# Gated products written in place in PSUM, and matrix comparisons moved to GpSimd, in an FNet plus PEER mixture-of-experts kernel

## The chip, the cores and the metric

The kernel runs on one core of a Trainium2 chip. A core has five engines that run their own instruction streams and meet at semaphores: TensorE (PE, with its weight loads shown as PEld), VectorE (DVE), ScalarE (ACT), GpSimd (POOL) and SyncE (SP, which here only issues DMAs). The measure is the device time of one execution in microseconds, lower being better.

## The reference

The kernel adds three things for 2048 tokens of width 512: the input, the real part of a two-dimensional Fourier transform of the layernormed input, and a mixture of 4096 one-row experts, of which every one of 32 heads picks two.

```python
def _A_ref(x, re_s, im_s, re_d, im_d):                 # FNet
    a = einsum("bsd,ed->bse", x, re_d); b = einsum("bsd,ed->bse", x, im_d)
    return einsum("ts,bse->bte", re_s, a) - einsum("ts,bse->bte", im_s, b)

def _B_ref(x, w_q, k1, k2, u, v):                      # PEER, K = 2, E = 64
    q = einsum("nd,dhc->nhc", xf, w_q)                 # 32 heads
    s1, s2 = q1 @ k1.T, q2 @ k2.T                      # 64 scores each
    # the two best of each half give four candidates, of which the two best are kept
    top_s, top_e = ...                                 # top_e = i1 * 64 + i2
    g = softmax(top_s)
    act = gelu(einsum("nd,nhkd->nhk", xf, u[top_e]))
    return einsum("nhk,nhk,nhkd->nd", g, act, v[top_e])

xn = layernorm(x)
return x + _A_ref(xn, ...) + _B_ref(xn, w_q, k1, k2, u, v)
```

The Fourier matrices are inputs. The kernel uses their symmetries to read only a part of them, so it also compares the parts it leaves out with the parts it uses, by subtracting mirrored pieces and summing absolute values; a flag at the end says whether the short way held. Another group of checks (`fit`) bounds the sizes of the expert tables, so that splitting them into two f16 halves is safe.

## The kernel before, in words

**First part (about 0 to 443 us).** Layernorm, the folded Fourier transform, the query product and the scores (line 796), and the top-two search on VectorE. Some of the matrix comparisons (numbers 8 to 23 and 40 to 51, the list `EARLY`) already lie here, on GpSimd. In this part the change only shifts line numbers.

**Expert part (about 443 to 1106 us).** The 2048 tokens are 16 tiles of 128. For 14 tiles, called blocks here, the kernel computes *all* 4096 experts densely and multiplies by a gate that is zero for experts that no head chose. The last two tiles are done by gathering only the chosen rows of the expert tables. One block b passes through these steps:

- `u_part` (line 956): z = u·x in eight groups (`cg` 0 to 7) of 48 matmuls into a PSUM tile. Groups 2 and 5 use the PSUM ring "pc", the others the ring "pb". ACT takes each group through gelu into the SBUF tile `act` (line 959).
- `g_mm` (lines 980 to 993): the gate of 32 tokens. VectorE builds two one-hot tiles `L` (line 980) and the weighted one-hot tile `R` (lines 988, 991), PE multiplies them (32 matmuls, line 993) into one PSUM gate tile `pg`. There are four such gates in a block (`tg` 0 to 3) and **two** `pg` buffers, so gate k+2 can be written only when gate k has been released.
- `w_part` (lines 1003 to 1016): VectorE multiplies `act`, a constant and the gate (line 1004) into the SBUF tile `w`. ACT rounds `w` to its f16 high half (line 1011), VectorE subtracts that from `w` for the low half (line 1014). High and low half replace `act` in place.
- `v_part` (line 1023): the eight groups of 12 matmuls that multiply the halves by the table v into one PSUM tile of the ring "pc"; `finish` (line 1038, VectorE) reads that tile into `y`, which frees it for group 2 or 5 of the next `u_part`.

A stage of PE is therefore: eight groups of z for block b with gates (b,0) and (b,1) among them, then eight groups of v for block b-1 with gates (b,2) and (b,3) among them. The small tables at the end of the program place the `w_part` steps: those of gates (b,0) and (b,1) go with groups 0 and 4 of v, those of (b,2) and (b,3) with groups 0 and 3 of the next z. The names z0 to z7 in this text are the groups of `u_part`; w0 to w3 the products of the four gates of a block, sub0 to sub3 the subtractions of line 1014, copy0 to copy3 the rounding of line 1011.

Three other chains are spread over these stages by counters (`pick` and `paced`), which issue a share of each list after each group of matmuls:

- the **row gathers** of the last two tiles: 128 steps, each an indirect DMA by POOL into a row buffer "ga" (line 1049, five buffers), a dot product on VectorE (line 1065), gelu and scaling on ACT (lines 1075, 1076, 1078), and an add on POOL (line 1083), after which POOL issues the next fetch into the freed buffer;
- the **late comparisons**: `compare` for the 36 numbers that are not in `EARLY`, and `compare_w` for four more. A comparison loads a 128x1024 tile "cx" by two SP DMAs, two steps later takes differences on VectorE (lines 739 to 773, by kind), and two steps after that ACT sums absolute values (lines 778, 780, called the judge below). Those with `g == 0` need a special treatment of row 0, hence extra small instructions on one partition;
- the `fit` checks on ACT (lines 1151, 1157).

The tiles "w", "cx" and "fit" of this part share one ring of four SBUF buffers (`WB`).

Every engine works strictly in the order of its own queue. That order is made by the scheduler of the framework out of the order in which the steps are written and their dependences.

Of the kernel before, what the change touches and what calls it, by code (L numbers as in the profile page):

```python
# [8 lines left out]
F32 = mybir.dt.float32  # L9
# [7 lines left out]
ALU = mybir.AluOpType  # L17
# [19 lines left out]
def tile_fnet_peer(ctx, tc, x, ca, cb, c5, wt, wf, wr, wq, kt, ut, vn, uv, out):  # L37
# [56 lines left out]
    early = cst.tile([P, len(EARLY)], F32, name="early")  # L94
    sums_sb = cst.tile([P, 138 + NF + 3], F32, name="sums")
    chk, asum = sums_sb[:, 0:70], sums_sb[:, 70:138]

# [3 lines left out]
    k16 = sums_sb[:, 0:128].bitcast(F16).rearrange("p (l w k) -> p l w k", l=2, w=2)  # L101
    fits = sums_sb[:, 138:]

# [452 lines left out]
    def part_b(safe, stS, stP, stE, xt, u_sb, cmp_p):  # L556
# [163 lines left out]
        def compare(n, at=None):  # L720
# [16 lines left out]
            def diff():  # L737
                if g == 0:
                    nc.vector.tensor_tensor(tv[:, 1], tv[:, 1], tv[:, 0], op=ops[0])
                    for i in (2, 3):  # L740
                        nc.vector.scalar_tensor_tensor(tv[:, i], tv[:, 0], not0, tv[:, i], op0=ALU.mult, op1=ops[i - 1])
                    f = (-1 if ri else 1) * sgn[1] * sgn[2]
                    nc.vector.tensor_tensor(tv[0:1, 3], tv[0:1, 3], tv[0:1, 2],
                                            op=ALU.subtract if f > 0 else ALU.add)
                else:
                    sets = {}
                    for i, o in enumerate(ops):
                        sets.setdefault(o, []).append(i + 1)
                    for o, ix in sets.items():
                        sl = slice(ix[0], ix[-1] + 1, ix[1] - ix[0] if len(ix) > 1 else 1)  # L750
                        v = tv[:, sl]
                        v_eng.tensor_tensor(v, v, tv[:, 0:1].to_broadcast([P, len(ix), 256]), op=o)
# [8 lines left out]

                if g == 0:
# [166 lines left out]
        TG = 32  # L929
        WB = 4  # L930
        BUFS = 5
        BT = [blk_tiles(b) for b in range(2)]
# [66 lines left out]
        def w_part(b, tg):  # L999
            act, _ = ACT[b]  # L1000
            ts = slice(tg * TG, (tg + 1) * TG)
            p = GP.pop((b, tg))
            w = bp.tile([P, NC, TG], F32, tag="w", name=f"w{b}_{tg}", bufs=WB)
            nc.vector.scalar_tensor_tensor(w, act[:, :, ts], fw,  # L1004
                                           p.rearrange("p h (n c) -> p c (h n)", c=NC),
                                           op0=ALU.mult, op1=ALU.mult)
            w16 = parts(b)[:, :, ts]
# [87 lines left out]
        def pick(after, k=1):  # L1095
            done[0] += k
            made = nc.cur_bb.bb.instructions
            for f in picks[done[1]:-(-len(picks) * done[0] // turns)]:
# [3 lines left out]
                for i in made[first:]:  # L1102
                    if i.engine in (mybir.EngineType.DVE, mybir.EngineType.Activation):
                        follow(i, after)
                    if i.engine == mybir.EngineType.Activation and after.ins.name in GL:
                        follow(i, GL[after.ins.name])

        def compare_w(n):

# [27 lines left out]
            if ri:  # L1137
                nc.scalar.activation(v[0][0:1, 0:P], v[0][0:1, 0:P], AF.Abs, accum_out=chk[0:1, 68 + half:69 + half])
            c = P - half
# [3 lines left out]
            f = t.rearrange("p k e -> p (k e)")[:, P - half * ri:]  # L1143
            after(2, lambda: nc.scalar.activation(f, f, AF.Abs, accum_out=chk[:, n:n + 1]))

# [16 lines left out]
        def verdict():  # L1162
# [3 lines left out]
            N = NF + 3  # L1166
            fm = sums_sb[:, 138 + NF:]
# [3 lines left out]
            cols = ((slice(0, 64), 50), (slice(64, 70), 47))  # L1171
            for i, (c, k) in enumerate(cols):
                nc.vector.tensor_reduce(fa[:, i:i + 1], asum[:, c.start:min(c.stop, 68)], axis=AX.X, op=ALU.add)
            nc.vector.tensor_scalar(bnd, bnd, -31.5, None, op0=ALU.add)
# [4 lines left out]
            follow(i.ins, T["a"])  # L1179
            k = nc.gpsimd.partition_all_reduce(fr[:, 2:], sums_sb[:, 138:], P, bass_isa.ReduceOp.absmax)  # L1180
            follow(k.ins, i)
# [39 lines left out]
        if not safe:  # L1221
            nc.vector.memset(chk[:, 68:70], 0.0)
            for k in range(0, len(EARLY), 16):
# [236 lines left out]
```

## Time and profile before

| what | us |
|---|---|
| median of three runs | 1119.79 (1116.18 to 1124.1) |
| profiled execution | 1113.87 |
| its span (first to last instruction) | 1112.1 |
| PE busy in the span | 1070.3 (96%) |
| VectorE busy | 996.7 (90%) |
| ACT busy | 717.7 (65%) |
| GpSimd busy | 640.3 (58%) |
| PE waiting for `y` (line 1038) | 15.5 |
| PE waiting for the gate product (line 1004) | 1.9 |

The profiled execution is 0.5% below the median. Busy times are sums over the whole span; the page of the profile also cuts the span into 40 slices, in which one reads that VectorE is at 0.9 or more of nearly every slice from 500 us on, and PE as well. A wait is put down to the instruction that ended it. Durations of matmuls are modelled, those of VectorE, ACT and POOL are records.

### The profile page before, as it was taken

To read this page: it belongs to the slowest core of one execution; us is meant where nothing else is said; L and a number is where in the kernel's file an instruction comes from. 1 tells how busy PE (TensorE), PEld (TensorE's weight loads), DVE (VectorE), ACT (ScalarE), POOL (GpSimd) and SP (SyncE) were. 2 spreads that over 40 slices of the span, in tenths; PEclk is the share of its full clock that TensorE was granted. 3 is DMA by queue.
4 is the path that set the end of the run, shared out by engine and by line. 5 is a ranking of instruction groups with operands and counts; after the bars stand their busy time and mean duration, and the time that the engine had idled before them with its cause. 6 is when DMAs were issued, how large, how long until landed. Compare 5 with 4: busy or idle time off the path is not lost. (4 is left out here: it accounts for less than half of the span.)

```text
span 1112.1 us, 28462 instructions
## 1 busy us (share of the span) xinstructions
PE 1070.3 (96%) x11070; PEld 700.6 (63%) x11070; DVE 996.7 (90%) x2786; ACT 717.7 (65%) x1324; POOL 640.3 (58%) x552
## 2 busy tenths in 40 slices
PE   5899999999999999999999999999998999999897
PEld 4355555454544544987695776968667686786853
DVE  6978897978999999987999999999999999998981
ACT  3576657778788767423766667767566666765660
POOL 0013537588797855211668677756666667667651
PEclk9899999999999999999999999999998999999899
DMA  8248153535446332553677577676767567776521
GB/s 326 83 172 284 49 198 113 173 125 198 153 153 206 106 114 65 186 158 109 186 213 238 193 212 231 225 232 201 215 199 209 182 214 237 230 222 189 158 67 51
DMA packets 84433, 196.72 MB, mean 177 GB/s; under 512 B 10294, under 2 KB 27069, under 8 KB 84288
## 3 DMA queue, kind: packets, MB, share of 16 engines
q1 hardware_dynamic: 63394, 123.49, 33.1%
q0 software_dynamic: 20736, 71.31, 21.8%
q8 instruction: 88, 1.44, 0.5%
q14 instruction: 57, 0.47, 0.1%
q10 hardware_dynamic: 158, 0.01, 0.0%
HBM read 177.68 MB, written 17.10 MB: 175 GB/s over the span
## 5 line engine op out<-in xcount | busy, mean ns | idle before, releaser
L796 PE MATMUL s<-m,xq 128*128 128x512 f16 x1536 | 338.9, 379 | 0.0
L956 PE MATMUL z<-xb,u 128*128 128x128 f16 x5376 | 313.9, 221 | 15.5 <-DVE y L1038 15.5
L956 PEld LDWEIGHTS <-u 128*128 128x128 f16 x5376 | 307.6, 99 | 19.2 <-issue 16.4
L1083 POOL TENSOR_TENSOR ov<-ov,ga 128x512 f32<-128x512 f32 x128 | 203.5, 1590 | 167.2 <-ACT ga L1078 145.7
L1023 PE MATMUL v<-v,act 128*128 128x512 f16 x1344 | 298.6, 379 | 0.0
L796 PEld LDWEIGHTS <-xq 128*128 128x128 f16 x1536 | 148.3, 98 | 171.4 <-issue 0.2
L1023 PEld LDWEIGHTS <-act 128*128 128x128 f16 x1344 | 128.3, 98 | 146.1
L1049 POOL DMA_INDIRECT ga<-in_uv_dram,eix x128 | 173.0, 1351 | 47.2 <-POOL ov L1083 34.2
L980 DVE TENSOR_TENSOR L<-io_lam,cmp 128x2048 f16<-128x2048 f16 x112 | 157.8, 1441 | 13.5 <-PE g L993 13.5
L804 DVE MAX8 vals<-ss 128x8 f32<-128x64 f32 x1024 | 152.4, 216 | 14.1 <-ACT ss L801 14.0
L959 ACT ACTIVATE act<-z,scl 128x512 f32<-128x512 f32 x112 | 75.8, 679 | 97.2 <-PE z L956 96.3
L808 DVE FIND_INDEX8 idx<-vals,ss 128x8 uint16<-128x256 f32 x256 | 107.1, 418 | 0.0
L801 ACT ACTIVATE ss<-s,wsc 128x512 f32<-128x512 f32 x112 | 75.5, 680 | 43.4 <-PE s L796 33.7
L1011 ACT ACTIVATE act<-w 128x1024 f16<-128x1024 f32 x56 | 75.5, 1348 | 43.3 <-DVE w L1004 39.8
L1078 ACT ACTIVATE ga<-ga,za 128x512 f32<-128x512 f32 x128 | 92.1, 721 | 9.8 <-ACT za L1076 0.4
L1014 DVE TENSOR_TENSOR act<-w,act 128x1024 f16<-128x1024 f32 x56 | 86.1, 1539 | 6.7 <-ACT act L1011 5.8
L778 ACT ACTIVATE cx<-cx 128x896 f32<-128x896 f32 x64 | 60.6, 946 | 40.3 <-DVE cx L758 12.9
L1065 DVE SCALAR_TENSOR_TENSOR ga<-ga,px 128x512 f32<-128x512 f32 x128 | 85.6, 676 | 0.1
L1004 DVE SCALAR_TENSOR_TENSOR w<-act,scl,g 128x1024 f32<-128x1024 f32 x56 | 70.9, 1271 | 0.4 <-ACT act L959 0.2
L169 POOL TENSOR_TENSOR wq<-wq,wh 128x1024 f16<-128x1024 f32 x26 | 55.4, 2134 | 24.4 <-ACT wq L166 23.7
L993 PEld LDWEIGHTS <-L 128*128 128x128 f16 x1792 | 52.2, 96 | 9.5 <-issue 2.7
L993 PE MATMUL g<-R,L 128*128 128x32 f16 x1792 | 54.0, 176 | 2.2 <-DVE w L1004 1.9
(274 smaller groups left out, 1312.4 us busy)
## 6 DMA issues: line engine op xcount, KB each, us to landing
cx<-in_cb_dram SPq DMA_DIRECT2D x64, 448.0 KB, 4.6
wq<-in_wq_dram SPq DMA_DIRECT2D x32, 512.0 KB, 5.8
fit<-in_wq_dram SPq DMA_DIRECT2D x28, 512.0 KB, 5.4
uv<-in_ut_dram SPq DMA_DIRECT2D x16, 512.0 KB, 4.1
uv<-in_vn_dram SPq DMA_DIRECT2D x16, 512.0 KB, 3.5
xq<-in_x_dram SPq DMA_DIRECT2D x8, 512.0 KB
xt_d<-xq SPq DMA_DIRECT2D x16, 256.0 KB, 3.0
cx<-in_ca_dram SPq DMA_DIRECT2D x64, 64.0 KB, 2.8
```

Source lines behind the costliest of these rows:

```text
L796: mm = nc.tensor.matmul(ps, xt[i][:, l, kd, :], m[:, r, kd, :], start=(n == 0), stop=(n == 3 * KD - 1))
L804: nc.vector.max(vals[:, i, w, :, h], s[:, g, :])
L808: nc.vector.max_index(idx[:, i, w].rearrange("p k h -> p (k h)"), vals[:, i, w, 0:2].rearrange("p k h -> p (k h)"), s[:, w * HC:g + 1, :]. ...
L956: mm = nc.tensor.matmul(p[:, cc * P:(cc + 1) * P], ug[:, l, c % 2, kd, :], xb[:, r, kd, :], start=(n == 0), stop=(n == 3 * KD - 1))
L980: nc.vector.tensor_tensor(L.rearrange("p t (l two) -> p t l two", two=2), io_lam.rearrange("p (l two) -> p l two", two=2).unsqueeze(1).to_ ...
L993: i = nc.tensor.matmul(p[:, hf, t * NC:(t + 1) * NC], L[:, t, :], R[:, hf * 16 + t, :], start=True, stop=True)
L1014: nc.vector.tensor_tensor(w16[..., 1], w, w16[..., 0], op=ALU.subtract)
L1023: mm = nc.tensor.matmul(pv, w16[:, c, :, l], vg[:, r, c % 2, :], start=(c == 0 and k == 0), stop=(c == NC - 1 and k == 2))
L1049: nc.gpsimd.indirect_dma_start(out=t, out_offset=None, in_=uv, in_offset=bass.IndirectOffsetOnAxis(ap=eix[:, n].rearrange("p k h -> p (k h ...
L1065: nc.vector.scalar_tensor_tensor(t, t, 1.0, T["x"], op0=ALU.mult, op1=ALU.mult, accum_out=T["z", n][:, s:s + 1])
L1078: nc.scalar.activation(t, t, AF.Copy, scale=z)
L1083: T["a"] = nc.gpsimd.tensor_tensor(o, o, t, op=ALU.add)
```

## The change

1. `w_part` no longer has an SBUF tile `w`. The product is written over the gate in PSUM. Line 1011 and line 1014 then read PSUM, and a gate buffer is in use until the subtraction of line 1014 is done.
2. `WB` goes from 4 to 3 and `BUFS` (row buffers "ga") from 5 to 6.
3. Of the 36 late comparisons 34 do their differences on GpSimd; numbers 0 and 32 stay on VectorE. The 14 with `g == 0` and `kk > 0` load rows 1 to 127 and, into partition 0, row 1 once more, by four DMAs in place of two, and then go the same way as the others: one instruction of 768 columns, or one of 512 and one of 256, and one of 128. Their rows 0 go to a new function `compare_r`, one tile for all of them: a memset on GpSimd, eight small DMAs, 14 small VectorE instructions on three or four partitions each, one sum on ACT. It is placed third in the list of comparisons.

Line numbers in the expert part move up by 3 in `compare` and `w_part` (1004 becomes 1007, 1014 becomes 1015 and so on).

```diff
-            v_eng = nc.vector if at is None else nc.gpsimd
+            v_eng = nc.vector if n % 32 == 0 else nc.gpsimd
...
-            nc.sync.dma_start(tf[:, :P], ca[ri, g, :, kk * P:(kk + 1) * P])
-            nc.sync.dma_start(tf[:, P:], cb[ri, g, kk].rearrange("p b c -> p (b c)"))
+            own = g == 0 and kk == 0
+            two = ((slice(1, P), slice(1, P)), (slice(0, 1), slice(1, 2)))
+            for e, a in two if g == 0 and kk else ((slice(0, P),) * 2,):
+                nc.sync.dma_start(tf[e, :P], ca[ri, g, a, kk * P:(kk + 1) * P])
+                nc.sync.dma_start(tf[e, P:], cb[ri, g, kk, a].rearrange("p b c -> p (b c)"))
...
-                if g == 0:
+                if own:
...
-        WB = 4
-        BUFS = 5
+        WB = 3
+        BUFS = 6
...
-            w = bp.tile([P, NC, TG], F32, tag="w", name=f"w{b}_{tg}", bufs=WB)
-            nc.vector.scalar_tensor_tensor(w, act[:, :, ts], fw,
-                                           p.rearrange("p h (n c) -> p c (h n)", c=NC),
-                                           op0=ALU.mult, op1=ALU.mult)
+            w = p.rearrange("p h (n c) -> p c (h n)", c=NC)
+            nc.vector.scalar_tensor_tensor(w, act[:, :, ts], fw, w, op0=ALU.mult, op1=ALU.mult)
...
+        def compare_r(n):
+
+            t = bp.tile([P, 4, 4, 64], F32, tag="w", name="cx_r", bufs=WB)
+            tf = t.rearrange("p s q c -> p (s q c)")
+            tv = t.rearrange("p s q c -> p s (q c)")
+            nc.gpsimd.memset(tf, 0.0)
+            cls = []
+            for c in range(4):
+                ri, odd = divmod(c, 2)
+                k0, k1 = (4, 8) if odd else (1, 4)
+                e = slice(32 * c, 32 * c + k1 - k0)
+                nc.sync.dma_start(tf[e, :P], ca[ri, 0, 0:1, k0 * P:k1 * P].rearrange("o (k f) -> (o k) f", f=P))
+                nc.sync.dma_start(tf[e, P:], cb[ri, 0, k0:k1, 0:1].rearrange("k o b c -> (k o) (b c)"))
+                cls.append((ri, odd, e))
+
+            def work():
+                for ri, odd, e in cls:
+                    sgn = (((1, 1, 1), (-1, 1, -1)), ((-1, -1, 1), (1, -1, -1)))[ri][odd]
+                    f = (-1 if ri else 1) * sgn[1] * sgn[2]
+                    m = ALU.add if ri else ALU.subtract
+                    nc.vector.tensor_tensor(tv[e, 1], tv[e, 1], tv[e, 0], op=ALU.subtract if sgn[0] > 0 else ALU.add)
+                    nc.vector.tensor_tensor(tv[e, 3], tv[e, 3], tv[e, 2], op=ALU.subtract if f > 0 else ALU.add)
+                    nc.vector.tensor_tensor(t[e, 0::2, 2:4], t[e, 0::2, 2:4], t[e, 0::2, 0:2], op=m)
+                    if odd and ri:
+                        nc.vector.tensor_copy(t[e, 2, 0:2], t[e, 0, 0:2])
+                    elif odd == ri:
+                        nc.vector.memset(t[e, 2, 0:2], 0.0)
+                after(2, lambda: nc.scalar.activation(tf[:, P:], tf[:, P:], AF.Abs, accum_out=chk[:, n:n + 1]))
+
+            after(2, work)
...
         units = [lambda n=n: (compare if n < 64 else compare_w)(n) for n in todo_n]
+        units.insert(2, lambda: compare_r(64))
```

What stands in the queues shows best how the work moves. First VectorE around products w0 and w1 of block 5, in the stage from 653 to 699 us of the trace before. `L_` and `R_` are the one-hot tiles, `g_0` and `g_1` the PSUM gates, `act` the activations, `ga` row buffers, `cx` a comparison's tile. Before:

```order
L980 TENSOR_TENSOR L_5792<-io_lam,cmp_9381 128x2048
L980 TENSOR_TENSOR L_5793<-io_lam,cmp_9381 128x2048
L988 TENSOR_TENSOR R_5795<-io_c,cmp_9381 128x1024
L991 TENSOR_TENSOR R_5795<-R_5795,cmp_9381 128x1024
L1065 SCALAR_TENSOR_TENSOR ga_38_9703,za_7124<-ga_38_9703,px_7123 128x512
L1004 SCALAR_TENSOR_TENSOR w_0_10044<-act_9377,scl,g_0_9661 128x1024
L1065 SCALAR_TENSOR_TENSOR ga_39_9768,za_7124<-ga_39_9768,px_7123 128x512
L1014 TENSOR_TENSOR act_9377<-w_0_10044,act_9377 128x32x32
L1065 SCALAR_TENSOR_TENSOR ga_40_9881,za_7124<-ga_40_9881,px_7123 128x512
L980 TENSOR_TENSOR L_5792<-io_lam,cmp_9381 128x2048
L980 TENSOR_TENSOR L_5793<-io_lam,cmp_9381 128x2048
L752 TENSOR_TENSOR cx_10068<-cx_10068 128x2x256
```

And with the change, from the same pair of one-hot tiles on:

```order
L983 TENSOR_TENSOR L_5792<-io_lam,cmp_9372 128x2048
L983 TENSOR_TENSOR L_5793<-io_lam,cmp_9372 128x2048
L991 TENSOR_TENSOR R_5795<-io_c,cmp_9372 128x1024
L994 TENSOR_TENSOR R_5795<-R_5795,cmp_9372 128x1024
L1066 SCALAR_TENSOR_TENSOR ga_38_9544,za_7117<-ga_38_9544,px_7116 128x512
L1007 SCALAR_TENSOR_TENSOR g_0_9651<-act_9368,scl,g_0_9651 128x32x32
L1007 SCALAR_TENSOR_TENSOR g_1_9920<-act_9368,scl,g_1_9920 128x32x32
L1066 SCALAR_TENSOR_TENSOR ga_39_9693,za_7117<-ga_39_9693,px_7116 128x512
L1015 TENSOR_TENSOR act_9368<-g_0_9651,act_9368 128x32x32
L1066 SCALAR_TENSOR_TENSOR ga_40_9755,za_7117<-ga_40_9755,px_7116 128x512
L983 TENSOR_TENSOR L_5792<-io_lam,cmp_9372 128x2048
L983 TENSOR_TENSOR L_5793<-io_lam,cmp_9372 128x2048
```

The comparison (cx) has left this queue, the second product (g_1) has moved up ahead of the first subtraction, and the subtraction is now the last reader of the gate tile g_0.

Second, GpSimd where the rows of gathers 34 to 36 are added (`ov` is the sum, `in_uv_dram` the table that is gathered from). Before:

```order
L1083 TENSOR_TENSOR ov_7195<-ov_7195,ga_34_9395 128x512
L1049 DMA ga_39_9768<-in_uv_dram,eix 128x1024
L1083 TENSOR_TENSOR ov_7195<-ov_7195,ga_35_9468 128x512
L1049 DMA ga_40_9881<-in_uv_dram,eix 128x1024
L1083 TENSOR_TENSOR ov_7195<-ov_7195,ga_36_9493 128x512
L1049 DMA ga_41_9976<-in_uv_dram,eix 128x1024
```

Adds and fetches alternate, each fetch five rows ahead of the add before it. With the change:

```order
L1084 TENSOR_TENSOR ov_7190<-ov_7190,ga_34_9351 128x512
L1050 DMA ga_40_9755<-in_uv_dram,eix 128x1024
L755 TENSOR_TENSOR cx_9747<-cx_9747 128x768
L761 TENSOR_TENSOR cx_9747<-cx_9747 128x128
L1084 TENSOR_TENSOR ov_7190<-ov_7190,ga_35_9386 128x512
L1050 DMA ga_41_9868<-in_uv_dram,eix 128x1024
L1084 TENSOR_TENSOR ov_7190<-ov_7190,ga_36_9462 128x512
L1050 DMA ga_42_9963<-in_uv_dram,eix 128x1024
```

The fetch is now six rows ahead, and a comparison's two instructions stand between a fetch and the next add.

Third, VectorE at the new tile `cx_r`, between the product of gate 2 and the subtraction of gate 1 of block 2 (the third block), where before there was no such tile:

```order
L1007 SCALAR_TENSOR_TENSOR g_2_7691<-act_6973,scl,g_2_7691 128x32x32
L1129 TENSOR_TENSOR cx_r<-cx_r 3x256
L1130 TENSOR_TENSOR cx_r<-cx_r 3x256
L1066 SCALAR_TENSOR_TENSOR ga_8_7414,za_7117<-ga_8_7414,px_7116 128x512
L1131 TENSOR_TENSOR cx_r<-cx_r 3x2x128
L1129 TENSOR_TENSOR cx_r<-cx_r 4x256
L1135 MEMSET cx_r 3x128
L1130 TENSOR_TENSOR cx_r<-cx_r 4x256
L1066 SCALAR_TENSOR_TENSOR ga_9_7478,za_7117<-ga_9_7478,px_7116 128x512
L1131 TENSOR_TENSOR cx_r<-cx_r 4x2x128
L991 TENSOR_TENSOR R_5794<-io_c,cmp_7785 128x1024
L1129 TENSOR_TENSOR cx_r<-cx_r 3x256
```

All of the small instructions are new in this place. Four more of them follow before the subtraction of gate 1, and two after it.

More of the change, by code (lines that the diff above doesn't have):

```diff
@@ L94, in tile_fnet_peer @@
     early = cst.tile([P, len(EARLY)], F32, name="early")
-    sums_sb = cst.tile([P, 138 + NF + 3], F32, name="sums")
-    chk, asum = sums_sb[:, 0:70], sums_sb[:, 70:138]
+    sums_sb = cst.tile([P, 139 + NF + 3], F32, name="sums")
+    chk, asum = sums_sb[:, 0:71], sums_sb[:, 71:139]
     wsc = cst.tile([P, 5], F32, name="wsc")
@@ L101, in tile_fnet_peer @@
     k16 = sums_sb[:, 0:128].bitcast(F16).rearrange("p (l w k) -> p l w k", l=2, w=2)
-    fits = sums_sb[:, 138:]
+    fits = sums_sb[:, 139:]
     hoff = cst.tile([P, HC], F32, name="hoff")
@@ L760, in mirror @@
                         v_eng.tensor_tensor(v[:, 3, 0:1], v[:, 3, 0:1], v[:, 2, 0:1], op=m)
-                if g == 0:
+                if own:
                     mirror(t[0:1, 2])
@@ L1137, in compare_w @@
             if ri:
-                nc.scalar.activation(v[0][0:1, 0:P], v[0][0:1, 0:P], AF.Abs, accum_out=chk[0:1, 68 + half:69 + half])
+                nc.scalar.activation(v[0][0:1, 0:P], v[0][0:1, 0:P], AF.Abs, accum_out=chk[0:1, 69 + half:70 + half])
             c = P - half
@@ L1143, in compare_w @@
             f = t.rearrange("p k e -> p (k e)")[:, P - half * ri:]
-            after(2, lambda: nc.scalar.activation(f, f, AF.Abs, accum_out=chk[:, n:n + 1]))
+            after(2, lambda: nc.scalar.activation(f, f, AF.Abs, accum_out=chk[:, n + 1:n + 2]))
         def fit(n):
@@ L1166, in verdict @@
             N = NF + 3
-            fm = sums_sb[:, 138 + NF:]
+            fm = sums_sb[:, 139 + NF:]
             fa = bp.tile([P, 2], F32, tag="fa", name="fa", bufs=1)
@@ L1170, in verdict @@
             o = bp.tile([1, 8], F32, tag="ok", name="ok", bufs=1)
-            cols = ((slice(0, 64), 50), (slice(64, 70), 47))
-            for i, (c, k) in enumerate(cols):
-                nc.vector.tensor_reduce(fa[:, i:i + 1], asum[:, c.start:min(c.stop, 68)], axis=AX.X, op=ALU.add)
+            cols = ((slice(0, 65), 50), (slice(65, 71), 47))
+            for i, c in enumerate((slice(0, 64), slice(64, 68))):
+                nc.vector.tensor_reduce(fa[:, i:i + 1], asum[:, c], axis=AX.X, op=ALU.add)
             nc.vector.tensor_scalar(bnd, bnd, -31.5, None, op0=ALU.add)
@@ L1179, in verdict @@
             follow(i.ins, T["a"])
-            k = nc.gpsimd.partition_all_reduce(fr[:, 2:], sums_sb[:, 138:], P, bass_isa.ReduceOp.absmax)
+            k = nc.gpsimd.partition_all_reduce(fr[:, 2:], sums_sb[:, 139:], P, bass_isa.ReduceOp.absmax)
             follow(k.ins, i)
@@ L1221, in part_b @@
         if not safe:
-            nc.vector.memset(chk[:, 68:70], 0.0)
+            nc.vector.memset(chk[:, 69:71], 0.0)
             for k in range(0, len(EARLY), 16):
```

## Prediction

> **What bounds the kernel now.** I read first the page's busy times, then who PE waits for, then the rows of PE in the expert part.
>
> ```profile
> PE 1070.3 (96%) x11070; PEld 700.6 (63%) x11070; DVE 996.7 (90%) x2786; ACT 717.7 (65%) x1324; POOL 640.3 (58%) x552
> PE z L956 <- DVE y L1038: 15.5, 6, 4.8
> PE g L993 <- DVE w L1004: 1.9, 1, 1.9
> ```
>
> PE sets the time, so the change can gain only what PE still waits for in the expert part, and loses whatever new waits it gives PE. The waits row by row, with two undisturbed stage starts:
>
> ```profile
> 565.05 2.84 PE L956 MATMUL z<-xb,u 128*128 128x128 f16 x48 [0.63 <-DVE y L1038]
> 613.45 2.84 PE L956 MATMUL z<-xb,u 128*128 128x128 f16 x48 [2.71 <-DVE y L1038]
> ...
> 653.61 8.20 PE L956 MATMUL z<-xb,u 128*128 128x128 f16 x144
> ...
> 699.14 8.20 PE L956 MATMUL z<-xb,u 128*128 128x128 f16 x144
> ...
> 798.40 4.09 PE L956 MATMUL z<-xb,u 128*128 128x128 f16 x48 [2.67 <-DVE y L1038]
> 849.38 5.19 PE L956 MATMUL z<-xb,u 128*128 128x128 f16 x48 [3.96 <-DVE y L1038]
> 898.29 2.84 PE L956 MATMUL z<-xb,u 128*128 128x128 f16 x48 [0.68 <-DVE y L1038]
> 1040.08 5.28 PE L956 MATMUL z<-xb,u 128*128 128x128 f16 x48 [4.84 <-DVE y L1038]
> 1067.48 0.95 PE L993 MATMUL g<-R,L 128*128 128x32 f16 x32 [1.92 <-DVE w L1004]
> ```
>
> A stage without a wait takes 699.14 - 653.61 = 45.53 us. Long waits also slow the group behind them: 48 matmuls take 2.84 us normally, but 4.09, 5.19 and 5.28 after three of the long ones. The first five waits cost 0.63 + 2.71 + 2.67 + 3.96 + 0.68 = 10.65, and 1.25 + 2.35 slow behind them: **14.3 us**. The last two, in the end region with `compare_w`, cost 4.84 + 2.44 + 1.92 = **9.2 us**. So 23.5 us is all there is to win.
>
> Why `y` is late: VectorE's queue is full. One stage, all work, then in the last row the comparisons (tile cx) alone, on VectorE, ACT and GpSimd:
>
> ```profile
> core 0: us, PE busy (x) PEld busy (x) DVE busy (x) ACT busy (x) POOL busy (x), PEclk, DMA share, GB/s
> 653.60:699.10 45.50, 45.50 (x612) 34.20 (x611) 43.33 (x56) 34.56 (x75) 30.76 (x22) 1.00 0.72 225
> ...
> 653.60:699.10 45.50, 8.51 (x7) 4.19 (x14) 0.00 (x0) 1.00 0.72 225
> ```
>
> VectorE is busy 43.33 of 45.50, GpSimd 30.76; 8.51 of VectorE's share is comparisons.
>
> **Part 1: comparisons leave VectorE.** Without them that stage has 43.33 - 8.51 = 34.82 us of VectorE work, so 10 us are free before `y`. I take all five early waits as gone: **-14.3 us**. What covers that: `y` had to be 0.6 to 4 us earlier, and a comparison is 3 to 4 us. Late next is the subject of part 2.
>
> **Part 2: the gate buffer is held longer.** PE's gate k+2 overwrites the buffer of gate k. Before, the product (L1004) released it; now the rounding on ACT and the subtraction (L1014) must be over too. In the old trace the subtraction comes *after* that moment (order of rows: PE gates; VectorE; ACT):
>
> ```profile
> 673.17 0.95 PE L993 MATMUL g<-R,L 128*128 128x32 f16 x32
> 684.42 0.95 PE L993 MATMUL g<-R,L 128*128 128x32 f16 x32
> 695.75 0.96 PE L993 MATMUL g<-R,L 128*128 128x32 f16 x32
> ...
> 671.13 1.34 DVE L1014 TENSOR_TENSOR act<-w,act 128x1024 f16<-128x1024 f32 x1
> 675.23 3.51 DVE L980 TENSOR_TENSOR L<-io_lam,cmp 128x2048 f16<-128x2048 f16 x2
> 681.67 1.27 DVE L1004 SCALAR_TENSOR_TENSOR w<-act,scl,g 128x1024 f32<-128x1024 f32 x1
> 684.36 1.36 DVE L1014 TENSOR_TENSOR act<-w,act 128x1024 f16<-128x1024 f32 x1 [0.81 <-ACT za L1075]
> 696.45 1.34 DVE L1014 TENSOR_TENSOR act<-w,act 128x1024 f16<-128x1024 f32 x1
> ...
> 690.77 0.81 ACT L699 ACTIVATE cmp<-zt 128x768 f16<-128x768 f16 x1 [0.74 <-PE zt L698]
> ```
>
> The gate at 684.42 would have waited until 684.36 + 1.36 = 685.72 (1.3 us), the one at 695.75 until 697.79 (2.0 us). Two such waits in every stage would be 3.3 us, or 36 us over eleven stages: the upper end. But the subtraction also moves earlier, since the comparisons ahead of it go. I redo both chains with mean durations:
>
> ```profile
> L980 DVE TENSOR_TENSOR L<-io_lam,cmp 128x2048 f16<-128x2048 f16 x112 | 157.8, 1441 | 13.5 <-PE g L993 13.5
> L1014 DVE TENSOR_TENSOR act<-w,act 128x1024 f16<-128x1024 f32 x56 | 86.1, 1539 | 6.7 <-ACT act L1011 5.8 <-ACT za L1075 0.8
> L1065 DVE SCALAR_TENSOR_TENSOR ga<-ga,px 128x512 f32<-128x512 f32 x128 | 85.6, 676 | 0.1
> L1004 DVE SCALAR_TENSOR_TENSOR w<-act,scl,g 128x1024 f32<-128x1024 f32 x56 | 70.9, 1271 | 0.4 <-ACT act L959 0.2
> L991 DVE TENSOR_TENSOR R<-R,cmp 128x1024 f16<-128x1024 f16 x56 | 47.9, 856 | 1.4
> L988 DVE TENSOR_TENSOR R<-io_c,cmp 128x1024 f16<-128x1024 f16 x56 | 45.7, 817 | 5.4 <-ACT cmp L699 5.4
> ...
> L980 DVE TENSOR_TENSOR L<-io_lam,cmp x112: 1197/1212/2876, 448.7 to 1072.7; 128x2048 f16<-128x2048 f16 x112
> ```
>
> *Gate (b,2)*: the first one-hot buffer is free when half of the earlier gate is done, 673.17 + 0.40 = 673.57. Then two L (2.88), two R steps (1.67), a dot (0.68), products w0 and w1 (2.54), a dot (0.68), the subtraction (1.34, an undisturbed one from the rows): 9.79 us, so 683.36, **1.06 us to spare**. With this stage's own L pair (3.51) it is 0.43. An L varies from 1.20 to 2.88 us, so a bad pair eats the rest.
>
> *Gate (b,3)*: R there needs the next block's `cmp`, which ends at 690.77 + 0.81 = 691.58 on ACT and follows PE's own progress. R steps 1.67, a dot 0.68, subtraction 1.34: 695.27, **0.48 to spare** against 695.75.
>
> *Gates (b,0), (b,1)*: for (b,1) the subtraction of 671.13 was over at 672.47, ahead of the gate at 673.17 even with the comparisons in the way. (b,0) needs ACT's rounding, which follows the gelu of z0 in ACT's queue; it is late only where a `fit` stands between, in about four stages of eleven.
>
> So three of four gates have margins of a half to one us in a queue whose pieces vary by over one. I put the mean wait at 0.4 (b,2), 0.4 (b,3) and 0.2 (b,0): 1.0 us a stage, eleven stages: **+11 us** (0 to 36). Each is too short to slow the matmuls behind it (after the waits of 0.63 and 0.68 they took 2.84).
>
> One row makes L the uncertain item: the same instruction takes 1.21 at the median and 2.88 at worst. [...]
>
> **Part 3: what stays on VectorE.** `compare_r` puts twelve small instructions between product w2 and the subtraction of gate 1 in one stage, number 32 stays, number 0 too. Nearest rows:
>
> ```profile
> L743 DVE TENSOR_TENSOR cx<-cx x16: 397/407/2161, 528.2 to 849.2; 1x256 f32<-1x256 f32 x16
> L739 DVE TENSOR_TENSOR cx<-cx 128x256 f32<-128x256 f32 x16 | 12.5, 781 | 0.0
> L741 DVE SCALAR_TENSOR_TENSOR cx<-cx,not 128x256 f32<-128x256 f32 x32 | 19.8, 659 | 0.0
> ```
>
> Twelve by 0.4 is 4.8 us, by the mean of the rows of line 739 nearer 9; gate (b,3) has 0.5 to spare, so PE waits some 4.5 us once, and runs slow behind it as it did after 3.96 (2.35 us): **+6.5 us**, by the row of the same width on few partitions, L743's median (0, if R's wait for `cmp` hides them; 10 by the dearer row). Number 32 stands ahead of `y`: 0.78 + 2 x 0.66 and smaller steps, some 3.5 us, like the comparisons that made `y` late before: **+3** (0 to 4). Number 0 **+1.7**, from the same rows with less behind it (0 to 4). At the start the gate (0,2) now waits for a subtraction: **+1.5**, one subtraction (0 to 3). In the end region `compare_w` stays on VectorE; its `y` wait shrinks, the gate there waits longer: **-1.8** (-9.2 to +4).
>
> **Part 4: GpSimd.** A comparison there, from those that ran on it in the first part, and its present work:
>
> ```profile
> L752 POOL TENSOR_TENSOR cx<-cx 128x512 f32<-128x512 f32 x20 | 25.5, 1274 | 2.8 <-DMA cx<-in_cb_dram 2.8
> L752 POOL TENSOR_TENSOR cx<-cx 128x256 f32<-128x256 f32 x20 | 14.7, 734 | 0.0
> L758 POOL TENSOR_TENSOR cx<-cx 128x128 f32<-128x128 f32 x24 | 10.9, 456 | 8.2 <-issue 6.9
> ...
> L1083 POOL TENSOR_TENSOR ov<-ov,ga 128x512 f32<-128x512 f32 x128 | 203.5, 1590 | 167.2 <-ACT ga L1078 145.7 <-ACT za L1075 6.8 <-DVE act L1014 5.9
> L1083 POOL TENSOR_TENSOR ov<-ov,ga x128: 1264/1299/6042, 521.9 to 1083.9; 128x512 f32<-128x512 f32 x128
> L1049 POOL DMA_INDIRECT ga<-in_uv_dram,eix x128 | 173.0, 1351 | 47.2 <-POOL ov L1083 34.2 <-DVE R L988 6.6 <-issue 1.5
> ```
>
> 1.27 + 0.73 + 0.46 = 2.46 us each; the list has 41 entries for 94 groups, eight groups a stage, so 3.5 a stage, 8.6 us. With the 30.76 and some 0.3 us between an add and its fetch (34.2 over 128 rows, about ten rows a stage: 562 us for 128) that makes 42.4 of 45.5; if comparisons stretch as the add does (1.590 on average, 1.299 at the median), 44.3. GpSimd stays just below the bound, its queue often late: the judge on ACT, two steps behind a comparison, waits for it, and behind the judge stand the row scaling and the rounding that releases the gate. The row chain has six buffers now, one step (about 4.4 us, 562 us for 128 rows) more for a late fetch. VectorE never waited for a gather (0.1 us at L1065), so that is worth nothing by itself. I take **+3** for the judge's delays (0 to 35).
>
> The 36 added DMA issues on SP stand two steps before their use and queue behind nothing PE reads: 0. The ring of three instead of four loses its 56 `w` tiles, more than a buffer's worth: 0.
>
> **Sum**: -14.3 + 11 + 6.5 + 3 + 1.7 + 1.5 - 1.8 + 3 = **+10.6 us** on the profiled 1113.87, so 1124.5; by the same step the median of 1119.79, which stands 0.5% higher, becomes about **1130**.
>
> **The rivals.**
>
> *Waits half as large.* The mean chains above leave room; if variation is smaller than I take it, part 2 is 4 us and `compare_r` 3: -14.3 + 4 + 3 + 3 + 1.7 + 1.5 - 1.8 + 3 = 0, **1120**. For it: the chains' means; against: L's spread.
>
> *The release is hidden, the `y` gain stays* (faster; decides if subtraction ends before PE's gate by over half a us in all stages). Parts 2 and 4 zero, `compare_r` 3, number 32 at 2, number 0 and the start together 1, the end region at -4: -14.3 + 3 + 2 + 1 - 4 = -12.3, **1107**. For it: 10 us freed on VectorE a stage; against: the -1.3 and -2.0 above, and R's wait for `cmp`.
>
> *GpSimd becomes the bound.* If adds, fetches and comparisons stretch by a further tenth, a stage needs 44.3 x 1.1 = 48.7, 3.2 us over PE's 45.5. VectorE's dots then wait for gathers and PE for VectorE: eleven stages +35, the waits of part 2 drown in it, part 3 stays at 12.7 and the early `y` gain at -14.3: +33 less what the end region catches up, **1151**. For it: single adds took up to 6.04 us; against: the 145.7 us that GpSimd now idles before the adds, waiting for ACT.
>
> *It doesn't do what it says*: the comparisons come back to VectorE as stretched one-hot builds. L's mean is 0.23 above its median, 112 times, 26 us beside 376 us of adds and fetches; 84 us more on GpSimd would add 6 us there and as much again on R and the rest, against some 8.5 a stage freed. Most of the relief stays; its price lies in the 1.0 us a stage above, and it has no chance of its own.
>
> **How the numbers follow.** Forecast as summed 0.45, half waits 0.2, hidden release 0.19, GpSimd bound 0.16. About 1% (11 us) is what a measurement of this kernel tells from no change. The forecast's own spread (1118 to 1143) lies about half above 1131, half within. So slower 0.23 + 0.16 = 0.39, within 0.22 + 0.2 = 0.42, faster 0.19. The range runs from the hidden release's 1105 to the GpSimd case's 1152.
>
> **What would show it.** After: waits `z <- y` small except one stage (number 32) and the end; new waits of PE's gate on the subtraction line, under 1 us, many, and one of some 5 us at `compare_r` in block 2's stage; VectorE near 40 of 45.5 in a stage, GpSimd 42 to 45. If GpSimd's comparisons take over 4 us each, or ACT's judge waits for them in most stages, I am too low; if no gate waits for the subtraction, too high.

## The result and the profile after

The changed kernel takes 1327.31 us (median, 1325.46 to 1327.56) against 1121.94 us of the kernel before on the same chip: a ratio of 1.182, 95% interval 1.175 to 1.190. It is 205 us slower, where the forecast was 10 us slower and the range ended at 1152.

The page of the changed kernel, its busy times, the slices of PE, of its granted clock and of the memory traffic, and the chain that ended last:

```profile
PE 1100.8 (83%) x11070; PEld 710.2 (54%) x11070; DVE 912.5 (69%) x2649; ACT 716.6 (54%) x1326; POOL 687.1 (52%) x652
...
PE   5899999999999999677447599965553579999998
...
PEclk9799999999999999898778699996786789999999
...
GB/s 277 74 266 120 180 117 170 144 180 143 203 89 128 59 241 88 118 144 77 80 146 102 140 248 217 205 101 105 119 88 122 98 180 219 218 199 232 185 75 43
...
PE 45%; SPq 19%; DVE 9%; DMA 9%; POOL 8%; issue 6%; ACT 3%; POOLq 0%; DVEq 0%; ACTq 0%
```

No engine is the bound any more. PE has two holes, slices 17 to 23 and 27 to 33 of 40, and the traffic is mostly 77 to 146 GB/s in both, so the memory is not busy with more work either. The last row, the chain, names the queue of SP with 19% and DMAs with 9%. (The chain on the old kernel's page covers only 4% of its span, so it can't be set beside this one; that of split112 in experiment 1, which differs from the changed kernel only in how these 14 loads are cut, has 1% and 6%.) Who waits for whom in these holes:

```profile
POOL cx L755 <- DMA cx<-in_cb_dram: 215.3, 14, 21.5
PE g L996 <- DVE act L1015: 183.7, 22, 31.7
ACT cx L781 <- POOL cx L761: 178.3, 22, 23.5
...
DVE act L1015 <- ACT act L1012: 110.0, 23, 18.1
...
ACT fit L1183 <- DMA fit<-in_wq_dram: 86.8, 6, 20.9
...
PE z L959 <- DVE y L1039: 13.1, 1, 13.1
```

Read from the top: GpSimd waits **fourteen** times for a comparison's load, 15 us on average. Fourteen is the number of comparisons with `g == 0` and `kk > 0`, the ones whose load was cut into 127 rows and one. ACT waits for GpSimd or for a `fit` load, VectorE's subtraction for ACT's rounding, PE's gate for the subtraction. PE's waits in the expert part went from 17.4 to 196.8 us, and its busy time rose by 30.5 us for the same 11070 matmuls: the granted clock (PEclk) goes down to 0.6 in and around the holes, where no slice of the old kernel was under 0.8. 179.4 + 30.5 = 210 of the 213.7 us by which the span grew.

One such place, the stage of block 3 (queues of SP, GpSimd, ACT, VectorE, PE in turn):

```profile
569.48 0.32 SPq L734 DMA_DIRECT2D cx<-in_ca_dram  x1
569.85 1.40 SPq L735 DMA_DIRECT2D cx<-in_cb_dram  x1
571.30 14.18 SPq L734 DMA_DIRECT2D cx<-in_ca_dram  x1
585.53 1.05 SPq L735 DMA_DIRECT2D cx<-in_cb_dram  x1
586.68 0.97 SPq L1182 DMA_DIRECT2D fit<-in_wq_dram  x2
...
599.89 1.80 POOL L755 TENSOR_TENSOR cx<-cx 128x768 f32<-128x768 f32 x1 [21.47 <-DMA cx<-in_cb_dram]
...
600.78 1.06 ACT L1183 ACTIVATE fit<-fit 128x1024 f32<-128x1024 f32 x1 [13.18 <-DMA fit<-in_wq_dram]
603.00 1.29 ACT L1012 ACTIVATE act<-g 128x1024 f16<-128x1024 f32 x1
...
604.32 1.30 DVE L1015 TENSOR_TENSOR act<-g,act 128x1024 f16<-128x1024 f32 x1 [16.54 <-ACT act L1012]
...
605.67 1.02 PE L996 MATMUL g<-R,L 128*128 128x32 f16 x32 [13.44 <-DVE act L1015]
```

SP issues the 127-row pieces (first two rows), and the next issue, a single row of 512 bytes, occupies SP for 14.18 us. Behind it stand the `fit` loads. The comparison's data is there 30 us after its issue, the `fit` data 14 us after theirs, where the `fit` loads of the old kernel landed 5.4 us after their issue (median; 6.3 at most). Then rounding, subtraction and gate follow within 5 us.

Where no such load runs, the changed kernel is as fast as the old one: from gate (5,0) at 769.24 us to gate (6,0) at 814.77 a stage takes 45.53 us, the length of an undisturbed stage before (columns as in the prediction's rows for one stage; GpSimd is the one with 38.07).

```profile
769.20:814.80 45.60, 45.60 (x617) 34.26 (x615) 37.51 (x47) 31.85 (x68) 38.07 (x32) 1.00 0.72 232
```

### The profile page after: what moved, and what is told of

It reads as the page before. It is cut to its first block, busy times and chain, and to the rows that moved or that the text cites. A ratio compares the mean times of both kernels' runs of the same rounds, so it can differ in the third digit from the quotient of the medians.

```text
span 1325.8 us, 28481 instructions
## 1 busy us (share of the span) xinstructions
PE 1100.8 (83%) x11070; PEld 710.2 (54%) x11070; DVE 912.5 (69%) x2649; ACT 716.6 (54%) x1326; POOL 687.1 (52%) x652
## 4 chain that ended last, share of the span: by engine, by line
PE 45%; SPq 19%; DVE 9%; DMA 9%; POOL 8%; issue 6%; ACT 3%; POOLq 0%; DVEq 0%; ACTq 0%
PE s L799 21%; SPq L734 10%; PE z L959 10%; SPq L735 8%; PE v L1024 8%; DMA fit<-in_wq_dram 5%; POOL ov L1084 3%; POOL ga L1050 2%; DMA cx<-in_cb_dram 2%; PE g L996 2%; POOL cx L755 2%; PE p L371 2%; PE m L147 1%; DVE vals L807 1%; DVE idx L811 1%
## 5 line engine op out<-in xcount | busy, mean ns | idle before, releaser
L959 PE MATMUL z<-xb,u 128*128 128x128 f16 x5376 | 316.9, 222 | 13.1 <-DVE y L1039 13.1
L959 PEld LDWEIGHTS <-u 128*128 128x128 f16 x5376 | 311.3, 100 | 16.6 <-issue 14.1
L1024 PE MATMUL v<-v,act 128*128 128x512 f16 x1344 | 318.8, 397 | 0.0
L755 POOL TENSOR_TENSOR cx<-cx 128x512 f32<-128x512 f32 (+2 forms) x109 | 122.8, 1144 | 228.7 <-DMA cx<-in_cb_dram 215.3
L1084 POOL TENSOR_TENSOR ov<-ov,ga 128x512 f32<-128x512 f32 x128 | 182.7, 1427 | 101.8 <-ACT ga L1079 85.6
L1024 PEld LDWEIGHTS <-act 128*128 128x128 f16 x1344 | 133.2, 101 | 160.9 <-issue 26.1
L996 PE MATMUL g<-R,L 128*128 128x32 f16 x1792 | 54.8, 179 | 187.1 <-DVE act L1015 183.7
L1050 POOL DMA_INDIRECT ga<-in_uv_dram,eix x128 | 148.6, 1161 | 47.1 <-POOL ov L1084 32.9
L1015 DVE TENSOR_TENSOR act<-g,act 128x1024 f16<-128x1024 f32 x56 | 72.6, 1298 | 125.8 <-ACT act L1012 110.0
L781 ACT ACTIVATE cx<-cx 128x896 f32<-128x896 f32 x64 | 60.6, 947 | 178.5 <-POOL cx L761 178.3
L991 DVE TENSOR_TENSOR R<-io_c,cmp 128x1024 f16<-128x1024 f16 x56 | 51.4, 919 | 89.0 <-ACT cmp L699 88.9
L1007 DVE SCALAR_TENSOR_TENSOR g<-act,scl,g 128x1024 f32<-128x1024 f32 x56 | 70.5, 1278 | 28.8 <-ACT act L962 26.0
## 6 DMA issues: line engine op xcount, KB each, us to landing
cx<-in_cb_dram SPq DMA_DIRECT2D x14, 444.5 KB
```

The lines of the kernel that those rows point to most:

```text
L959: mm = nc.tensor.matmul(p[:, cc * P:(cc + 1) * P], ug[:, l, c % 2, kd, :], xb[:, r, kd, :], start=(n == 0), stop=(n == 3 * KD - 1))
L996: i = nc.tensor.matmul(p[:, hf, t * NC:(t + 1) * NC], L[:, t, :], R[:, hf * 16 + t, :], start=True, stop=True)
L1024: mm = nc.tensor.matmul(pv, w16[:, c, :, l], vg[:, r, c % 2, :], start=(c == 0 and k == 0), stop=(c == NC - 1 and k == 2))
L1050: nc.gpsimd.indirect_dma_start(out=t, out_offset=None, in_=uv, in_offset=bass.IndirectOffsetOnAxis(ap=eix[:, n].rearrange("p k h -> p (k h ...
L1084: T["a"] = nc.gpsimd.tensor_tensor(o, o, t, op=ALU.add)
```

## The experiments

Theory A: a transfer of 127 rows runs at a fraction of the usual speed and holds up what stands behind it. Theory B: the loss is that of a gate buffer held until the subtraction, with GpSimd now in the chain to it. Ratios are to the kernel before, run on the same chip in the same session, with 95% intervals.

### 1. The same change with 112 + 16 rows

```diff
-            two = ((slice(1, P), slice(1, P)), (slice(0, 1), slice(1, 2)))
+            two = ((slice(16, P), slice(16, P)), (slice(0, 16), slice(1, 17)))
```

> The changed kernel, but the 14 comparisons of g = 0, kk > 0 are loaded as rows 16 to 127 into their partitions and rows 1 to 16 into partitions 0 to 15 (112 + 16 rows) in place of 127 + 1; four DMAs as before. Theory A (a transfer of 127 rows runs at a fraction of the speed, and everything behind it on SP's queue and on that part of the DMA engines is late): GpSimd's wait for the cx load falls from 215 us to under 10, SP's issues from 14 us to under 2.5, and the time lands where the rest of the change puts it, 1105 to 1140 us. Theory B (the gate buffer that is held until the subtraction, with GpSimd in the chain to it, makes the loss): still over 1250 us.

Measured: **1121.76 us**, ratio 1.0032 (1.0008 to 1.0056). Nothing else differs from the changed kernel, and 205.5 us are gone (200 by the two ratios); what is left over the kernel before is some 4 us. PE's waits in this run:

```profile
PE g L996 <- DVE act L1015: 21.1, 16, 8.0
...
PE g L996 <- DVE fa L1205: 3.2, 1, 3.2
```

(In the second row one gate at the end waits for the sums of the checks.) GpSimd's wait for these loads falls from 215.3 to 0.7 us, and no SP issue on lines 734 and 735 took more than 2.47 us. Theory B falls: the gate buffer is still held until the subtraction, with GpSimd's comparisons as they were, and PE waits 21.1 us for it, not 183.7.

### 2. How the time goes with the number of rows

The same line with `slice(6, P)` and `slice(0, 6)` from rows 1 to 6 (122 + 6 rows), and with `slice(2, P)` and `slice(0, 2)` (126 + 2).

> The same with 122 + 6 rows. If the shape alone matters (a row count that does not divide over the 16 DMA engines), theory A has two engines for the 122 rows: a load takes about half of the 15 to 20 us of the 127-row load, most of it before its use two steps later (about 11 us), so 1125 to 1220 us, between split112 and the changed kernel. If only the odd first partition matters, it is like split112 within 1%. Theory B: over 1250 us.

> The changed kernel with 126 + 2 rows per load. 126 is no multiple of 16 either, but has the divisor 14. If a transfer is spread over the largest number of engines up to 16 that divides its rows (127: 1, 122: 2, 126: 14, 112: 16): within 1% of split112, 1115 to 1132 us, and no SP issue over 3 us. If every row count that is no multiple of 16 is slow, like split122 or worse: over 1180 us.

| rows in the large piece | largest divisor up to 16 | median us | ratio | longest SP issue, line 735 |
|---|---|---|---|---|
| 127 | 1 | 1327.31 | 1.182 (1.175 to 1.190) | 12.22 |
| 122 | 2 | 1186.89 | 1.061 (1.056 to 1.065) | 9.74 |
| 126 | 14 | 1122.28 | 1.004 (1.001 to 1.006) | 1.91 |
| 112 | 16 | 1121.76 | 1.003 (1.001 to 1.006) | 2.47 |

The longest issues of line 734 go the same way: 14.46, 4.74, 0.78 and 0.79 us. An odd first partition or a count that is no multiple of 16 is not what costs: the 122 rows begin at partition 6 and still lose 65 us against 112, while 126 rows are as good as 112. In these four runs the time follows the divisor, as the first case of split126's expectation has it: at 1 and 2 it is 1327.31 and 1186.89 us, at 14 and 16 it is 1122.28 and 1121.76. GpSimd's longest wait for such a load goes with it, 21.5 us at 127 rows, 10.0 at 122, 2.9 at 126. The traces do not number the engines, so how many of them carry a transfer was not shown; only for 127 rows is there a measured share: while such transfers run alone in experiment 4, the mean busy share of the 16 DMA engines is 0.06, and 16 x 0.06 = 0.96, the work of about one engine.

### 3. The loads alone, in the old kernel

```diff
-            nc.sync.dma_start(tf[:, :P], ca[ri, g, :, kk * P:(kk + 1) * P])
-            nc.sync.dma_start(tf[:, P:], cb[ri, g, kk].rearrange("p b c -> p (b c)"))
+            two = (slice(1, P), slice(0, 1))
+            for e in two if g == 0 and kk else (slice(0, P),):
+                nc.sync.dma_start(tf[e, :P], ca[ri, g, e, kk * P:(kk + 1) * P])
+                nc.sync.dma_start(tf[e, P:], cb[ri, g, kk, e].rearrange("p b c -> p (b c)"))
```

> The kernel before, with nothing changed but the same 14 tiles loaded as rows 1 to 127 and row 0 apart, by four DMAs (the same data). Theory A: VectorE in place of GpSimd waits for these loads, and the fit checks too, over 100 us together; 1270 to 1340 us. Theory B: 1115 to 1130 us, as before.

Measured: **1335.01 us**, ratio 1.195 (1.189 to 1.200). The old kernel, same data, same arithmetic, comparisons on VectorE, loses as much as the changed one (the intervals of the two ratios touch). Its waits:

```profile
DVE cx L741 <- DMA cx<-in_cb_dram: 237.5, 14, 21.6
...
ACT fit L1153 <- DMA fit<-in_wq_dram: 70.7, 5, 20.4
```

The same fourteen waits, now on VectorE. So the loss needs neither the product in place nor GpSimd.

### 4. Its own slow load, or the others held up?

A comparison waits for its load, but `fit` loads wait too. Fourteen further transfers that nobody reads were added to split112:

```diff
+            if at is None and g == 0 and kk:
+                dm = dram.tile([P, 8 * P], F32, name=f"dm{n}")
+                nc.sync.dma_start(dm[1:P, P:], cb[ri, g, kk, 1:P].rearrange("p b c -> p (b c)"))
```

> split112 with 14 further transfers of 127 rows (the same 444.5 KB pieces, into DRAM scratch that nobody reads), one behind each of the 14 loads on SP's queue. If the loss comes from the comparison waiting for its own slow load: 1118 to 1135 us, since nothing waits for these. If it comes from the slow transfer holding up others (SP's issue and the part of the DMA engines that it occupies): fit loads and comparisons wait behind it, 1220 to 1330 us.

Measured: **1348.64 us**, ratio 1.205 (1.201 to 1.209), but not as it was meant. Having no dependences, all 14 were scheduled at the start, one behind the other:

```profile
L738 SPq DMA_DIRECT2D dm<-in_cb_dram x14: 628/17293/17294, 48.4 to 248.7; - x14
```

```profile
ACT wh L161 <- DMA wq<-in_wq_dram: 224.4, 1, 224.4
```

Between 100 and 200 us no compute engine does anything, and only these transfers run (the last two numbers are the mean busy share of the DMA engines and GB/s):

```profile
100.00:200.00 100.00, 0.00 (x0) 0.00 (x0) 0.00 (x0) 0.00 (x0) 0.00 (x0) 0.50 0.06 26
```

That is the price by itself: back to back, one 444.5 KB piece (455,168 bytes, here into DRAM) per 17.29 us, 26 GB/s, against 4.6 us from issue to landing for the 448 KB piece of the old kernel. And the first part's weight load, an ordinary 128-row transfer, waited 224 us behind them. Pinned to their places behind each load (`follow(d.ins, ld)`):

> dummy_127 with each dummy transfer pinned behind the load that it stands after, so that they run in the expert part instead of at the start, where the scheduler had put all 14. If holding up others is enough (nobody reads the dummies): SP issues of over 10 us, ACT waits for fit loads, PE for the gate's subtraction, 1240 to 1340 us. If the comparison's own slow load is needed for the loss: 1118 to 1150.

Measured: **1287.63 us**, ratio 1.150 (1.146 to 1.155).

```profile
ACT fit L1187 <- DMA fit<-in_wq_dram: 165.9, 11, 37.2
PE g L1000 <- DVE act L1019: 141.1, 18, 28.7
...
PE z L963 <- DMA xb<-xt_d: 11.5, 1, 11.5
```

Nobody reads these transfers, every comparison has its load of 112 + 16 rows, and still 166 us are lost against split112, some 12 a transfer. Holding up others is enough. In SP's queue one sees it directly: in twelve of the fourteen places the next issue behind a dummy takes 3.5 to 18.4 us, in the other two under 2. Two of the places (the last row is two issues, the first of which took 10.70 us):

```profile
525.31 0.67 SPq L738 DMA_DIRECT2D dm<-in_cb_dram  x1
532.38 3.69 SPq L1186 DMA_DIRECT2D fit<-in_wq_dram  x1
...
569.55 0.61 SPq L738 DMA_DIRECT2D dm<-in_cb_dram  x1
570.25 11.79 SPq L1186 DMA_DIRECT2D fit<-in_wq_dram  x2
```

### 5. What the rest of the change is worth

Each half alone. First the product in place in the old kernel, comparisons on VectorE (the `w_part` lines of the change, `WB = 3`, `BUFS = 6`):

> The kernel before with the product written over the gate in PSUM, WB = 3 and BUFS = 6, the comparisons staying on VectorE as they were. By the margins of the old trace (the subtraction 1.3 and 2.0 us after PE's gate, in most stages) PE waits for it 1.5 to 3.3 us a stage: theory A 1130 to 1160 us. Theory B: over 1200 us.

Measured: **1134.63 us**, ratio 1.015 (1.010 to 1.020). PE waits 28.3 us for the subtraction in 21 places, and the waits for `y` are gone, although the comparisons are still on VectorE. So the held buffer alone costs more than it gives.

```profile
PE g L993 <- DVE act L1012: 28.3, 21, 3.3
```

Then split112 with the product back in SBUF (`WB = 4`, `BUFS = 5`), the comparisons on GpSimd:

> split112 with the product back in an SBUF tile of its own (WB = 4, BUFS = 5), so the gate is free after the product again; the comparisons stay on GpSimd. If the waits for the subtraction are a cost of the in-place product alone (21 us in split112, of which 8 at compare_r), PE waits for nothing in the expert part but the end: 1096 to 1108 us. If they would be replaced by waits for VectorE at the same place (one-hot builds held up by GpSimd's comparisons): 1114 to 1125.

Measured: **1135.96 us**, ratio 1.015 (1.011 to 1.019). I had expected 1096 to 1108 if the in-place product was a pure cost. Both ranges were too low. The other reading is the nearer one, since PE waits for VectorE again, but less at the gates (7.0 us), as it said, than for `y`: those waits are back, though the comparisons have left VectorE.

```profile
PE z L959 <- DVE y L1041: 22.6, 9, 6.5
...
PE g L996 <- DVE w L1007: 7.0, 3, 4.2
...
DVE ga L1068 <- DMA ga<-in_uv_dram,eix: 21.6, 6, 7.4
```

What the two differ in shows in VectorE's subtraction, first with its input in SBUF, then in PSUM (split112), from the two runs' groups:

```profile
L1017 DVE TENSOR_TENSOR act<-w,act 128x1024 f16<-128x1024 f32 x56 | 104.6, 1870 | 15.4 <-ACT act L1014 11.4 <-ACT za L1078 3.8
```

```profile
L1015 DVE TENSOR_TENSOR act<-g,act 128x1024 f16<-128x1024 f32 x56 | 72.8, 1301 | 17.9 <-ACT act L1012 17.8
```

With both inputs in SBUF it takes 1.87 us on average beside GpSimd's comparisons (1.54 in the old kernel, with the comparisons on VectorE). With one input in PSUM it takes 1.30, never more than 1.33, and it is 1.30 in inplace_only too, so there it makes no difference where the comparisons run. Between the two runs that is 32 us of VectorE's queue. Each half alone loses 1.5%; together they are at +0.3%. With the comparisons on GpSimd the waits for the subtraction fall from 28.3 to 13.1 us (`compare_r` apart), and the product in PSUM keeps those comparisons from slowing the subtraction. Other instructions are still slowed by them: the two steps of R took 117.2 us in split112, and 93.6 in the old kernel and 91.7 in inplace_only, where the comparisons are on VectorE.

In w_in_sbuf VectorE also waited 21.6 us for gathers, with five row buffers. Whether the buffers did that:

```diff
-        BUFS = 6
+        BUFS = 5
```

> split112 with five row buffers in place of six. By the prediction (six buffers are worth nothing) 1119 to 1125 us; if the 21.6 us that VectorE waited for gathers in w_in_sbuf (five buffers) came from the buffers, and not from the product's place, VectorE waits 10 to 25 us for gathers here too and the time is 1127 to 1140.

Measured: **1123.57 us**, ratio 1.005 (1.003 to 1.007), its interval overlapping that of split112; VectorE waited 2.5 us for gathers. The sixth buffer is worth at most a few tenths of a per cent here, and five buffers alone do not make the 21.6 us. GpSimd being late in w_in_sbuf is the likelier cause (its comparisons averaged 1.36 us there, 1.17 in split112), but no run shows it by itself.

### 6. The tile of rows 0

In split112 the one long wait of PE is where the prediction put it:

```profile
553.24 1.30 DVE L1129 TENSOR_TENSOR cx_r<-cx_r 3x256 f32<-3x256 f32 x1
...
563.47 2.71 DVE L1130 TENSOR_TENSOR cx_r<-cx_r 4x256 f32<-4x256 f32 x1
566.21 1.28 DVE L1015 TENSOR_TENSOR act<-g,act 128x1024 f16<-128x1024 f32 x1
...
567.55 1.04 PE L996 MATMUL g<-R,L 128*128 128x32 f16 x32 [7.96 <-DVE act L1015]
```

From the first small instruction to the subtraction 13 us pass, with single ones stretched to 2.7 us from 0.41. Without `compare_r` (`units.insert(2, ...)` removed; this leaves out the comparison of those rows 0):

> split112 without compare_r (it leaves out the comparison of rows 0 of the 14 matrices pieces). The gate (2,3) then does not wait 8 us: 1111 to 1116 us if that wait is on the path for its full length; 1119 to 1123 if it only hides other waits.

Measured: **1125.28 us**, ratio 1.005 (1.003 to 1.008). That is a little above both ranges. The wait of 7.96 is gone, the longest is 3.2, and the sum of the waits for the subtraction is 22.8 instead of 21.1. With one entry fewer the list of comparisons is spread otherwise, and other gates wait. Moving the small instructions to GpSimd:

> split112 with the small instructions of compare_r on GpSimd. The 8 us wait of gate (2,3) goes: 1111 to 1117 us if that is a net gain; by what no_row0 showed (the wait gone, the time not) 1119 to 1127.

Measured: **1123.94 us**, ratio 1.005 (1.002 to 1.007). The wait only moved: gate (3,0) at 579.77 now waits 7.78 us. ACT, which sums this tile, first waited 15.27 us for GpSimd's small instructions, and the rounding for that gate stands behind the sum in ACT's queue. And with the product in SBUF:

> w_in_sbuf with the small instructions of compare_r on GpSimd. With the product in SBUF they are not in the chain to the gate any more, so this should be within 0.3% of w_in_sbuf; if they still hold up y or a one-hot build, 3 to 6 us faster than it.

Measured: 1139.79 us, ratio 1.019 (1.016 to 1.022); no gain over w_in_sbuf. No version that was run beats the kernel before.

## Why the prediction was wrong

- **The step that failed** is the sentence "The 36 added DMA issues on SP stand two steps before their use and queue behind nothing PE reads: 0." I counted the added issues and not what the cut does to the loads: each of the 14 loads now has two pieces of 127 rows, 63.5 and 444.5 KB. They cost 205.5 us (1327.31 less 1121.76, 14.7 us a load), more than the 197 us by which the forecast of 1130 was off. "Queue behind nothing" looks the wrong way: what costs is what queues behind *them*, and that is everything on SP's queue, `fit` loads, `xb`, `y`. The sum did say slower, but by terms that come to some 4 us in split112; that the result is slower is no merit of theirs.
- The old trace had shown it. A 127-row load of 508 KB stands in its first part, at line 277, and the issue behind it, one row, takes as long as those that made the loss:

```profile
16.97 0.30 SPq L277 DMA_DIRECT2D c<-in_ca_dram  x1
18.31 13.82 SPq L278 DMA_DIRECT2D c<-in_ca_dram  x1
```

- No rival covered it. The GpSimd rival had the right engine in a wait, but with 1151 us for the wrong reason: GpSimd is at 38 of 45.6 us in a clean stage, and idle in the holes.
- **Part 1**, -14.3 us: no wait for `y` is left in split112, but not by the mechanism given, so this was luck. The waits for `y` are gone in inplace_only too, with the comparisons still on VectorE, and back at 22.6 us in w_in_sbuf, with the comparisons on GpSimd. In the four kernels they go with the place of the product, not with that of the comparisons. Why was not taken apart: with an input in PSUM the subtraction is shorter (1.30 us in split112, 1.87 in w_in_sbuf), and PE is already held at the gate. VectorE's instructions already ran longer beside GpSimd's in the old trace (a first step of R took 1.76 us at 678.66 beside an add on GpSimd, 0.68 at 668.60 with none). That the comparisons there would give time back in this way was mentioned and set too low: L took 6.8 us more in split112 (6 foreseen), but the two steps of R 23.6 ("as much again" foreseen).
- **Part 2**, +11 us of short waits: in split112 the waits for the subtraction are 21.1 us in all, less 7.96 at `compare_r` and 0.81 at the start leaves 12.3 us. The mechanism and the size were right, though the number of places (14) is smaller and each is longer (0.9 on average, 1.9 at most).
- **Part 3**: `compare_r` 7.96 us for 6.5 foreseen, but not worth that much in the end, since no_row0 is no faster. Numbers 32 and 0 cost nothing that shows (3 and 1.7 foreseen). The start cost 0.81 (1.5). In the end region the waits of 4.84 and 1.92 are gone and one of 3.2 is new (-1.8 foreseen).
- **Part 4**: GpSimd was at 41.0 of 45.5 us in the stage from 653.6 of split112, 42.4 to 44.3 foreseen; it did not become the bound. Six buffers were worth nothing that could be told. The sign "ACT's judge waits for them in most stages" did show in split112 (20 times, 49.4 us) and cost nothing that shows there; in the changed kernel it grew to 178.3 us because GpSimd itself waited for its loads.

```profile
653.60:699.10 45.50, 45.14 (x611) 33.91 (x609) 37.79 (x46) 33.35 (x73) 41.03 (x33) 1.00 0.73 232
```

- The sum without the failed step was +10.6 us; split112 measured +3.6 (ratio 1.0032, 1 to 6 us), between the forecast and the rival of "waits half as large" at 0.

## What to carry to other kernels

When an edit cuts a load into pieces, look at the row count of each piece before counting issues: here 127 rows took nearly four times as long as a 128-row load (17.29 us back to back, against 4.6 from issue to landing) and held up what stood behind them on the queue (the next issue took 14.18 us in the stage shown first), while 112 + 16 rows, or 126 + 2, cost nothing that shows. Before calling a new transfer free, look in the old trace for one of the same shape, and at the issue *behind* it. And two edits that lose 1.5% each by themselves lost only 0.3% together: try the halves apart and together before judging either.

## What was not expected of the hardware

- A transfer of 127 rows and 444.5 KB took 17.29 us back to back, 26 GB/s (dummy_127). The next issue of the same queue took 3.5 to 18.4 us in twelve of fourteen places (dummy_in_place), and up to 14.46 us where it carried one row (the changed kernel).
- It slows ordinary 128-row transfers too: `fit` loads were waited for 165.9 us in dummy_in_place, where nobody reads the slow ones. Both SP's queue and the time from issue to landing have a part in it: in the stage shown first, SP was held for 14.18 us, and the `fit` loads, once issued, landed 14 us later in place of 5.4. How the loss divides between the two was not taken apart; a run with the slow transfers on another queue would tell.
- A VectorE subtraction of 128x1024 took 1.28 to 3.70 us (mean 1.87) with both inputs in SBUF beside GpSimd's work (w_in_sbuf), and 1.27 to 1.33 with one in PSUM (split112).
